# Second MLP product by seven block products (Strassen's algorithm), with the block sums on VectorE and GpSimd and a new order of the work

## The chip, the cores and the metric

One core of a Trainium2 chip. The metric is the device time of one execution in microseconds (us). Weights and inputs come from HBM, the output goes back to HBM, all inside the timed execution.

## The reference

A gated linear attention with 8 heads of 48, followed by a normalisation and a two-layer MLP, over 4 batches of 768 positions, all in float32:

```
B, H, S, D = 4, 8, 768, 48
f = 1 / (1 + exp(-f_logit))
for t in range(S):
    state = f[t] * state + outer(k[t], v[t])     # per batch and head, 48 x 48
    y[t] = q[t] @ state
x = y as (B, S, H*D)                             # 384 columns
xn = (x - mean(x)) / sqrt(var(x) + 1e-6) * g_ln
out = x + maximum(xn @ w_ch1, 0) @ w_ch2         # 384 -> 1536 -> 384
```

Almost all the arithmetic is in the two products of the last line. w_ch1 and w_ch2 arrive as float64 and are turned into float32 in the kernel.

## The kernel before

**Units.** The 768 positions are cut into 12 units of 64 positions. A unit holds these 64 positions of all 4 batches, so 256 rows for the MLP, as two groups of 128 (index g). `attention(n)` and `mlp(n)` are Python generators. A token `a3.scores` in a plan runs the attention of unit 3 up to its stage "scores", a token `m2` runs the next step of the MLP of unit 2, `l3q` issues the loads of q for unit 3. Every engine executes its instructions in the order in which the plan emits them: there is no scheduler, the plan's text alone sets the order. The plan START covers units 0 and 1 with the reading of the weights, and then UNIT is run for m = 2 to 11, which emits the MLP of unit m together with the attention of unit m+1 and the loads of unit m+2.

**The attention of a unit** on TensorE (PE): transposes of f, k and q (`tr`, line 541 in the profile), products with the carried state (`py<-kept`, L615), scores (`ps`, L626), transposes of k (`kp`, L639), products with v (`py<-v`, L649), the new state (`pn`, L674), and the transposes of the normalised rows (`xp`, L703). VectorE (DVE) runs two scans (`after`, `upto`), the products `kh`, `qh`, `kept`, the masked scores `sc`, the statistics `stats`/`mv`, the new `state` and the normalised rows `xn`; GpSimd (POOL) makes the reciprocal deviation `rstd`; ScalarE (ACT) makes the sigmoid `gates` and the copies `kt`, `x`, `xt` out of PSUM.

**The MLP of a unit.** The first product `ph` (L718): for each pair of the 12 blocks of 128 hidden columns, six matmuls with 256 moving columns, and a ReLU on ScalarE into `h` (L720). The second product `po` (L725): for each of the two groups g, twelve matmuls with `h[:, i, g]` as weights and `w2[:, i]` (384 columns) as moving data into one PSUM bank; VectorE then adds x (`o`, L730) and SyncE (SP) issues two stores. In the profile each float32 matmul is recorded as two passes, each with its own weight load (LDWEIGHTS, shown as PEld): 72 matmuls of `ph` and 48 of `po` in a unit.

**The weights.** Each of the 12 pieces (6 of w1, 6 of w2) is fetched by one DMA of 768 KB (token `f`, tile `words`), read by three ScalarE instructions (`r`, L501 to L503, tiles `upper` and `units`), and put together by three VectorE instructions and one GpSimd instruction (`w`, L511 to L518). Pools of rotating buffers: `words` has three, `upper` and `units` two each. PSUM: four single banks, taken in rotation by `tr`, `ph`, `kp`, `po` and `xp`, and two double banks for `py`, `ps` and `pn`. f, q and k have two tiles each, units taking them in turns.

Of the kernel before, what the change touches and what calls it, by code (L numbers as in the profile page):

```python
# [302 lines left out]


START = """
l0v f l0k l0q l0x f l1k l1f a0.gates l1q a0.after a0.k_across a0.upto
a0.k f a0.q a0.scores r a0.causal l1v l1x w a0.kt a0.values r a0.stats
w a1.gates a0.state a0.norm a0.turn m0 r a1.after f a1.k_across f a1.upto
a1.k a1.q w f f r m0 a1.scores a1.causal a1.kt r a1.values
f w w a1.stats r f a1.state m0 m0 r m0 w  # L310
a1.norm l2k a1.turn w m0 m1 r f m1 m1 m1 w
r w r f f r l2f w l3q m1 l2q w
m0 m1 r l2v l2x m0 w a2.gates m1 a2.after m0 m0 a2.k_across
a2.upto a2.k m0 a2.q m1 a2.scores l3k a2.causal l3v l3x l3f a2.kt m1
a2.values m0 a2.stats a2.state m1 a2.norm m1 a2.turn m1
"""
UNIT = """
m{m} a{n}.gates a{n}.after
m{m} a{n}.k_across a{n}.upto
m{m} a{n}.k  # L320
m{m} a{n}.q l{o}f l{o}k l{o}q l{o}v l{o}x
m{m}
m{m} a{n}.scores a{n}.causal a{n}.kt
m{m}
m{m} a{n}.values a{n}.stats a{n}.state
m{m}
m{m} a{n}.norm
m{m} a{n}.turn
m{m}
"""  # L330


# [1 line left out]
def kernel(  # L334
# [58 lines left out]
    def one_bank(name):  # L393
        return ps1.tile([P, 512], FP32, tag="one", name=name)
# [3 lines left out]

    wide_heads = {}
    for name, fill in (("f", 40.0), ("q", 0.0), ("k", 0.0)):  # L400
        for i in range(2):
            t = consts.tile([P, G, H, 64], FP32, name=f"{name}raw{i}")
            nc.gpsimd.memset(t[:, :, :, D:64], fill)
            wide_heads[name, i] = t
    loaded = {}

    def load(n, name, engines=(nc.sync,)):
        if n >= NU:
            return
        if name == "x":  # L410

            loaded[n, name] = raws.tile([P, G, NP, D], FP32, tag="rawx", name=f"vx{n}")
            odd = v.rearrange("b (a r) s d -> b r s a d", r=2)
            for b in range(B):
                nc.sync.dma_start(out=loaded[n, name][(1 - b % 2) * T:(2 - b % 2) * T, b // 2],
                                  in_=odd[b, 1, n * T:(n + 1) * T])
            return
        if name == "v":
            vt = raws.tile([P, G, H, D], FP32, tag="rawv", name=f"v{n}")
            loaded[n, name] = vt  # L420
        else:
            loaded[n, name] = wide_heads[name, n % 2]
        src = {"f": f_logit, "k": k, "q": q, "v": v}[name]
        for b in range(B):
            engines[b % len(engines)].dma_start(  # L425
                out=loaded[n, name][(b % 2) * T:(b % 2 + 1) * T, b // 2, :, 0:D],
                in_=src[b, :, n * T:(n + 1) * T, :].rearrange("h p d -> p h d"))
# [64 lines left out]
    def read():  # L492
# [1 line left out]
        if not fetched:  # L494
            return
        name, words, to, r, w = fetched.pop(0)
        upper = stage.tile([P, r, w], FP32, tag="upper", bufs=2, name=f"{name}upper")
        units = stage.tile([P, r, w], FP32, tag="units", bufs=2, name=f"{name}units")
        wv = words.rearrange("p r (f two) -> p two r f", two=2)
        low, high = wv[:, 0].bitcast(U32), wv[:, 1].bitcast(FP32)  # L500
        nc.scalar.activation(out=upper, in_=high, func=AF.Copy, scale=2.0 ** -112)  # L501
# [17 lines left out]

    pairs = [(g, a) for g in range(G) for a in range(NP)]
    x_of, norm_of, xt_of = {}, {}, {}

    def half(i):
        return slice(64 * i, 64 * i + 64)
# [170 lines left out]
    def turn(n):  # L697
# [8 lines left out]
                              mul=gain[:, m:m + 1])  # L706
        xt_of[n] = xt

    def mlp(n):

        x = x_of.pop(n)
        xt = xt_of.pop(n)
        h = work.tile([P, KF, W], FP32, tag="h", bufs=2, name=f"h{n}")
        for i in range(0, KF, 2):
            ph = one_bank(f"ph{n}").rearrange("p (i t) -> p i t", i=2)
            for j in range(2):
# [2 lines left out]
                                     rhs=xt[:, m], start=m == 0, stop=m == KD - 1)  # L719
            nc.scalar.activation(out=h[:, i:i + 2], in_=ph, func=AF.Relu)  # L720
            yield
        for g in range(G):
            po = one_bank(f"po{n}")[:, 0:DM]
            for i in range(KF):
                nc.tensor.matmul(po, lhsT=h[:, i, g * P:(g + 1) * P], rhs=w2[:, i],  # L725
                                 start=i == 0, stop=i == KF - 1)
                if i % 4 == 3 and i < KF - 1:
                    yield
            o = xs.tile([P, DM], FP32, tag="o", bufs=2, name=f"o{n}")
            nc.vector.tensor_tensor(out=o, in0=x[:, g], in1=po, op=ALU.add)  # L730
            for b in range(2):
                nc.sync.dma_start(out=out[2 * g + b, n * T:(n + 1) * T, :], in_=o[half(b)])
            yield

# [5 lines left out]
    def run(plan):  # L740
        for token in plan.split():
# [9 lines left out]
            elif kind == "m":  # L751
                if token not in running:
                    running[token] = mlp(int(rest))
                next(running[token])
            elif kind == "l":
                load(int(rest[:-1]), rest[-1])
            else:
                {"r": read, "w": write, "f": fetch}[token]()

    run(START)  # L760
    assert not (queue or fetched or opened)
# [48 lines left out]
```

## Time and profile before

| | |
|---|---|
| time, median of 3 runs | 515.3 us (514.0 to 515.7) |
| profiled execution | 515.5 us, its span 513.7 us |
| PE busy | 485.0 us, 94% of the span |
| PEld (weight loads) | 369.7 us, 72% |
| DVE, ACT, POOL busy | 200.7, 129.8 and 41.8 us (39%, 25%, 8%) |
| mean granted TensorE clock | 0.985 |

The busy time of an engine is the union of its instructions. The chain of work that ended last is followed back from the last instruction, at each step to what released it; its shares add up to the span. The table by stretches gives busy times between two points of the span, and the timeline lists instructions in order: start, duration, engine, line, output<-input, shapes, count, and in brackets the idle time of that engine before and what ended it.

### The profile page before, as it was taken

How to read it: one execution, taken by the hardware profiler on the slowest of the kernel's cores; microseconds unless marked ns; L12 is line 12 of the kernel's file. 1: busy time of each engine (PE TensorE's matmuls, PEld its weight loads, DVE VectorE, ACT ScalarE, POOL GpSimd, SP SyncE). 2: the span in 40 equal slices, each digit the busy share in tenths (PEclk: the TensorE clock that was granted, in tenths of full speed). 3: DMA queues.
4: the chain of work that ended last, by engine and by line, in shares of the span. 5: the costliest groups of instructions: out<-in, count | busy, mean ns of one | idle time of the engine just before them, and what ended most of it. 6: DMA issues, size and time to landing. Idle time of an engine off the chain costs nothing.

```text
span 513.7 us, 10940 instructions
## 1 busy us (share of the span) xinstructions
PE 485.0 (94%) x4841; PEld 369.7 (72%) x4841; DVE 200.7 (39%) x285; ACT 129.8 (25%) x255; POOL 41.8 (8%) x53
## 2 busy tenths in 40 slices
PE   2698896999999999999999999999999999999995
PEld 1487783668867867867877876876876876876862
DVE  5879557543432431531521621612603512522000
ACT  3358673012212112212112111221211211211100
POOL 3214326000000000000000000000000000000000
PEclk9969999999999999999999999999999999999999
DMA  9977667433402502602601701700700610000001
GB/s 170 169 197 252 138 155 108 93 63 65 90 14 55 103 3 58 112 3 49 121 3 39 130 4 32 133 7 22 137 14 17 131 25 17 17 1 17 17 1 36
DMA packets 122760, 36.20 MB, mean 70 GB/s; under 512 B 115792, under 2 KB 118864, under 8 KB 122704
## 3 DMA queue, kind: packets, MB, share of 16 engines
q1 hardware_dynamic: 121248, 35.21, 33.9%
q8 instruction: 40, 0.66, 0.5%
q10 hardware_dynamic: 1456, 0.20, 0.3%
q14 instruction: 16, 0.13, 0.1%
HBM read 30.67 MB, written 4.72 MB: 69 GB/s over the span
## 4 chain that ended last, share of the span: by engine, by line
PE 87%; DVE 5%; SPq 3%; issue 1%; ACT 1%; DMA 1%; POOL 1%; DVEq 0%; POOLq 0%
PE po L725 35%; PE ph L718 34%; PE tr L541 6%; SPq L425 3%; PE py L615 2%; PE py L649 2%; PE pn L674 2%; PE ps L626 2%; PE kp L639 2%; PE xp L703 1%; DVE w_0body L514 1%; DMA fraw<-in_f_logit_dram 1%; POOL w L518 1%; DVE w_0body L511 1%; DVE w_0upper L516 1%
## 5 line engine op out<-in xcount | busy, mean ns | idle before, releaser
L725 PE MATMUL po<-w,h 128*128 128x384 f32 x576 | 195.2, 492 | 4.0 <-POOL w L518 4.0
L718 PE MATMUL ph<-xt,w 128*128 128x256 f32 x864 | 195.1, 381 | 0.7 <-ACT xt L705 0.7
L718 PEld LDWEIGHTS ph<-xt,w 128*128 128x128 f32 x864 | 162.8, 191 | 24.3 <-issue 1.1
L725 PEld LDWEIGHTS po<-w,h 128*128 128x128 f32 x576 | 107.4, 191 | 72.8 <-POOL w L518 5.2
L720 ACT ACTIVATE h<-ph 128x512 f32<-128x512 f32 x72 | 42.8, 596 | 166.2 <-PE ph L718 166.2
L730 DVE TENSOR_TENSOR o<-x,po 128x384 f32<-128x384 f32 x24 | 13.3, 554 | 117.6 <-PE po L725 117.6
L555 DVE TENSOR_TENSOR_SCAN after<-gates,ends 128x1040 f32<-128x1040 f32 (+1 forms) x13 | 28.0, 2155 | 35.7 <-ACT gates L574 35.7
L705 ACT ACTIVATE xt<-xp,gain 128x128 f32<-128x128 f32 x72 | 20.0, 375 | 82.9 <-PE xp L703 82.9
L663 DVE BATCH_NORM_STATS2 stats<-x 128x6 f32<-128x384 f32 x24 | 13.0, 543 | 58.9 <-ACT x L659 58.9
L630 DVE TENSOR_TENSOR sc<-ps,causal 128x1024 f32<-128x1024 f32 x12 | 14.7, 1225 | 53.0 <-PE ps L626 53.0
L665 POOL TENSOR_SCALAR rstd<-mv 128x2 f32<-128x2 f32 x12 | 2.8, 234 | 369.0 <-DVE mv L664 368.9
L567 DVE TENSOR_TENSOR_SCAN upto<-gates,starts 128x1040 f32<-128x1040 f32 (+1 forms) x13 | 28.1, 2158 | 0.5
L641 ACT COPY kt<-kp 128x512 f32<-128x512 f32 x24 | 12.9, 589 | 45.1 <-PE kp L639 45.1
L659 ACT COPY x<-py 128x384 f32<-128x384 f32 x24 | 10.3, 482 | 54.1 <-PE py L649 54.1
L593 DVE TENSOR_TENSOR qh<-tr,upto 128x512 f32<-128x512 f32 x24 | 15.6, 686 | 21.0 <-PE tr L541 21.0
L541 PE MATMUL tr<-ident,fraw 128*128 128x128 f32 x96 | 14.7, 298 | 8.5 <-DMA fraw<-in_f_logit_dram 8.5
L541 PEld LDWEIGHTS tr<-ident,fraw 128*128 128x128 f32 x96 | 12.2, 154 | 10.5 <-issue 4.4
L518 POOL TENSOR_TENSOR w<-w_0upper,w_0units 128x768 int32<-128x768 int32 x7 | 15.5, 2212 | 35.5 <-DVE w_0upper L516 19.5
L541 PE MATMUL tr<-ident,kraw 128*128 128x128 f32 x96 | 13.6, 286 | 5.1 <-DMA kraw<-in_k_dram 4.9
L649 PEld LDWEIGHTS py<-v,sc 64*64 64x64 f32 x384 | 12.3, 134 | 7.7 <-issue 6.6
L593 DVE TENSOR_TENSOR kh<-tr,after 128x512 f32<-128x512 f32 x24 | 15.3, 677 | 4.0 <-PE tr L541 4.0
L541 PEld LDWEIGHTS tr<-ident,kraw 128*128 128x128 f32 x96 | 11.7, 148 | 7.1 <-DMA kraw<-in_k_dram 5.3
(90 smaller groups left out, 335.3 us busy)
## 6 DMA issues: line engine op xcount, KB each, us to landing
w_0words<-in_moe_w_ch_dram SPq DMA_DIRECT2D x7, 768.0 KB, 5.2
v<-in_v_dram SPq DMA_DIRECT2D x48, 96.0 KB, 3.0
kraw<-in_k_dram SPq DMA_DIRECT2D x48, 96.0 KB, 3.1
qraw<-in_q_dram SPq DMA_DIRECT2D x48, 96.0 KB, 3.1
out_dram<-o SPq DMA_DIRECT2D x48, 96.0 KB, 2.2
fraw<-in_f_logit_dram SPq DMA_DIRECT2D x46, 96.0 KB, 3.2
vx<-in_v_dram SPq DMA_DIRECT2D x48, 48.0 KB, 2.5
w_256words<-in_moe_w_ch_dram SPq DMA_DIRECT2D x1, 768.0 KB, 5.2
```

What stands on the lines that cost most here:

```text
L425: engines[b % len(engines)].dma_start(out=loaded[n, name][(b % 2) * T:(b % 2 + 1) * T, b // 2, :, 0:D], in_=src[b, :, n * T:(n + 1) * T, : ...
L518: nc.gpsimd.tensor_tensor(out=to.bitcast(I32), in0=upper, in1=units, op=ALU.add)
L541: nc.tensor.transpose(pt[:, a * P:(a + 1) * P], src[:, g, 2 * a:2 * a + 2].rearrange("p h e -> p (h e)"), ident)
L555: nc.vector.tensor_tensor_scan(out=after.rearrange(flat)[:, c0:c1][:, ::-1], data0=gt[:, c0 + 1:c1 + 1][:, ::-1], data1=ends.rearrange(fla ...
L567: nc.vector.tensor_tensor_scan(out=upto.rearrange(flat)[:, c0:c1], data0=gt[:, c0:c1], data1=starts.rearrange(flat)[:, c0:c1], initial=0.0 ...
L593: nc.vector.tensor_tensor(out=dst[:, segs], in0=pt, in1=by[:, segs, 1:E1], op=ALU.mult)
L630: nc.vector.tensor_tensor(out=sc.rearrange("s r e t -> s (r e) t"), in0=ps.rearrange("s r e t -> s (r e) t"), in1=causal.unsqueeze(1).broa ...
L649: nc.tensor.matmul(py[half(b), r, e * D:(e + 1) * D], lhsT=sc[rows, r, e], rhs=vx[rows, g, a] if r else vt[rows, g, 2 * a], start=n == 0 a ...
L705: nc.scalar.mul(out=xt[:, m, g * P:(g + 1) * P], in_=pt[:, m], mul=gain[:, m:m + 1])
L718: nc.tensor.matmul(ph[:, j], lhsT=w1[:, m, (i + j) * P:(i + j + 1) * P], rhs=xt[:, m], start=m == 0, stop=m == KD - 1)
L720: nc.scalar.activation(out=h[:, i:i + 2], in_=ph, func=AF.Relu)
L725: nc.tensor.matmul(po, lhsT=h[:, i, g * P:(g + 1) * P], rhs=w2[:, i], start=i == 0, stop=i == KF - 1)
```

## The change

With h as a 2 x 2 matrix of blocks a11, a12 (group 0, first and second six hidden blocks) and a21, a22 (group 1), and w2 as b11, b12 (first six hidden blocks, left and right 192 columns) and b21, b22, the second product is formed from seven block products in place of eight (Winograd's form of Strassen's algorithm). The sums of weights `mixed` (t1 to t4) are made once, in three parts, on VectorE (token `t`). The sums of h (token `s`: s1, s2, s4, and s3 written over a21) are made for each unit on VectorE. Each product is six matmuls with 192 moving columns (`product`, one PSUM bank each); VectorE adds it, GpSimd adds the partial sums to x, and four tiles of 192 columns (`p1x`, `u4y`, `u4x`, `u2x`) are stored with two DMAs each. f, q and k have one tile each, the pools `raws` and `stage` (with `words`) two buffers instead of three, and START and UNIT are written anew; the MLP of a unit now has 13 steps in place of 12.

```
-    raws = fast.enter_context(tc.tile_pool(name="raws", bufs=3))
-    stage = fast.enter_context(tc.tile_pool(name="stage", bufs=3))
+    raws = fast.enter_context(tc.tile_pool(name="raws", bufs=2))
+    stage = fast.enter_context(tc.tile_pool(name="stage", bufs=2))
...
-            loaded[n, name] = wide_heads[name, n % 2]
+            loaded[n, name] = wide_heads[name]
...
+    def mix():
+        rows = slice(to_mix[0], to_mix.pop(0) + 2)
...
+        for to, x1, x2 in ((t1, b12, b11), (t2, b22, t1), (t3, b22, b12), (t4, t2, b21)):
+            nc.vector.tensor_tensor(out=to, in0=x1, in1=x2, op=ALU.subtract)
...
+    def sums(n):
...
+        nc.vector.tensor_tensor(out=s1, in0=a21, in1=a22, op=ALU.add)
+        nc.vector.tensor_tensor(out=s2, in0=s1, in1=a11, op=ALU.subtract)
+        nc.vector.tensor_tensor(out=a21, in0=a11, in1=a21, op=ALU.subtract)
+        nc.vector.tensor_tensor(out=s4, in0=a12, in1=s2, op=ALU.subtract)
...
-        for g in range(G):
-            po = one_bank(f"po{n}")[:, 0:DM]
-            for i in range(KF):
-                nc.tensor.matmul(po, lhsT=h[:, i, g * P:(g + 1) * P], rhs=w2[:, i],
...
+        def product(name, a, b):
+            pp = one_bank(f"p{name}_{n}")[:, 0:CH]
+            for i in range(KH):
+                nc.tensor.matmul(pp, lhsT=a[:, i], rhs=b[:, i], start=i == 0, stop=i == KH - 1)
+            return pp
...
+        nc.scalar.copy(out=p1, in_=product("p1", a11, b11))
+        add(nc.gpsimd, p1x, p1, x[:, 0, left])
+        yield
+        add(nc.vector, p1x, p1x, product("p2", a12, b21))
+        put(p1x, 0, left)
+        yield
+        s1, s2, s3, s4 = sums_of.pop(n)
+        add(nc.vector, p1, p1, product("p6", s2, t2))
+        add(nc.gpsimd, u2x, p1, x[:, 1, left])
+        yield
+        add(nc.vector, p1, p1, product("p5", s1, t1))
+        add(nc.gpsimd, u4x, p1, x[:, 0, right])
+        add(nc.gpsimd, u4y, p1, x[:, 1, right])
+        yield
+        p7 = product("p7", s3, t3)
+        add(nc.vector, u2x, u2x, p7)
+        add(nc.vector, u4y, u4y, p7)
+        put(u4y, 1, right)
+        yield
+        add(nc.vector, u4x, u4x, product("p3", s4, b22))
...
+        add(nc.vector, u2x, u2x, product("p4", a22, t4), ALU.subtract)
```

**PE, the second product of unit 2 behind the scores of unit 3.** The number after a name's first letters is the unit. Before, from the new state of unit 3 onward:

```order
L674 MATMUL pn3_1419<-v3_1010,kt3_1353 64x48 x32
L725 MATMUL po2_1366<-w2_60,h2_1166 128x384 x4
L725 MATMUL po2_1461<-w2_60,h2_1166 128x384 x8
L703 MATMUL xp3_1474<-ident_58,xn3_1466 128x128 x3
L703 MATMUL xp3_1481<-ident_58,xn3_1466 128x128 x3
L725 MATMUL po2_1461<-w2_60,h2_1166 128x384 x4
```

In the changed kernel, from the product p5 onward:

```order
L753 MATMUL pp5_2_1544<-mixed1_121,s1_2_1466 128x192 x6
L753 MATMUL pp7_2_1560<-mixed3_123,h2_1285 128x192 x6
L683 MATMUL pn3_1571<-v3_1255,kt3_1429 64x48 x32
L753 MATMUL pp3_2_1612<-w2_60,s4_2_1468 128x192 x6
L712 MATMUL xp3_1623<-ident_58,xn3_1609 128x128 x3
L712 MATMUL xp3_1630<-ident_58,xn3_1609 128x128 x3
L753 MATMUL pp4_2_1637<-mixed4_124,h2_1285 128x192 x6
```

Between the new state `pn3` and the transposes `xp3` there were twelve matmuls of 384 columns (four and eight); there is now one product of six matmuls of 192 columns.

**DVE, the same place.** Before, from the masked scores of unit 3 to the second addition of x:

```order
L630 TENSOR_TENSOR sc3_1351<-ps3_1318,causal_111 128x1024
L663 BN_STATS stats3_1408<-x3_1407 128x6
L664 BN_AGGR mv3_1409<-stats3_1408 128x2
L663 BN_STATS stats3_1408<-x3_1407 128x6
L664 BN_AGGR mv3_1409<-stats3_1408 128x2
L679 TENSOR_TENSOR state_126<-kept3_1245,pn3_1419 128x768
L730 TENSOR_TENSOR o2_1457<-x2_1077,po2_1366 128x384
L693 TENSOR_SCALAR xn3_1466<-x3_1407,mv3_1409,rstd3_1410 128x384 x2
L730 TENSOR_TENSOR o2_1492<-x2_1077,po2_1461 128x384
```

In the changed kernel the four sums and the additions of p2 and p6 stand between `sc3` and the first row here:

```order
L761 TENSOR_TENSOR p1_2_1473<-p1_2_1473,pp5_2_1544 128x192
L672 BN_STATS stats3_1539<-x3_1538 128x6
L673 BN_AGGR mv3_1540<-stats3_1539 128x2
L672 BN_STATS stats3_1539<-x3_1538 128x6
L673 BN_AGGR mv3_1540<-stats3_1539 128x2
L761 TENSOR_TENSOR u2x_2_1475<-u2x_2_1475,pp7_2_1560 128x192
L761 TENSOR_TENSOR u4y_2_1477<-u4y_2_1477,pp7_2_1560 128x192
L688 TENSOR_TENSOR state_120<-kept3_1346,pn3_1571 128x768
L702 TENSOR_SCALAR xn3_1609<-x3_1538,mv3_1540,rstd3_1541 128x384 x2
L761 TENSOR_TENSOR u4x_2_1476<-u4x_2_1476,pp3_2_1612 128x192
L761 TENSOR_TENSOR u2x_2_1475<-u2x_2_1475,pp4_2_1637 128x192
```

The statistics now stand behind the addition of p5, and `state` and `xn` behind the two additions of p7.

**SP, the fetches in START.** Before, from the fourth piece of w1 on:

```order
L489 DMA w10_768words_418<-in_moe_w_ch1_dram 128x3x512
L489 DMA w10_1024words_430<-in_moe_w_ch1_dram 128x3x512
L489 DMA w10_1280words_459<-in_moe_w_ch1_dram 128x3x512
L489 DMA w20_0words_461<-in_moe_w_ch2_dram 128x2x768
L489 DMA w22_0words_600<-in_moe_w_ch2_dram 128x2x768
L489 DMA w24_0words_623<-in_moe_w_ch2_dram 128x2x768
L425 DMA kraw0_94<-in_k_dram 64x8x48 x4
L489 DMA w26_0words_742<-in_moe_w_ch2_dram 128x2x768
```

In the changed kernel:

```order
L480 DMA w10_768words_396<-in_moe_w_ch1_dram 128x3x512
L480 DMA w10_1024words_398<-in_moe_w_ch1_dram 128x3x512
L480 DMA w10_1280words_437<-in_moe_w_ch1_dram 128x3x512
L480 DMA w20_0words_568<-in_moe_w_ch2_dram 128x2x768
L416 DMA kraw_90<-in_k_dram 64x8x48 x4
L480 DMA w22_0words_612<-in_moe_w_ch2_dram 128x2x768
L480 DMA w24_0words_614<-in_moe_w_ch2_dram 128x2x768
L416 DMA fraw_86<-in_f_logit_dram 64x8x48 x4
L480 DMA w26_0words_633<-in_moe_w_ch2_dram 128x2x768
```

The order of the pieces is the same; the loads of k and f of unit 2 stand two pieces, respectively three pieces, earlier, and a piece now waits for the piece two before it to be read, where it waited for the piece three before.

More of the change, by code (lines that the diff above doesn't have):

```diff
@@ L713, in mlp @@
         h = work.tile([P, KF, W], FP32, tag="h", bufs=2, name=f"h{n}")
+        h_of[n] = h
         for i in range(0, KF, 2):
@@ L721, in mlp @@
             yield
[L722 to L733 removed]
+        left, right = slice(0, CH), slice(CH, DM)
```

80 lines of the change are left out of this document (50 added, 30 removed).

## The prediction

> **What bounds the kernel now.** I read the table by stretches first: the start, a unit in the middle (unit 3, between its first `ph` and that of unit 4), the unit with the last attention, and the last unit.
>
> ```profile
> core 0: us, PE busy (x) PEld busy (x) DVE busy (x) ACT busy (x) POOL busy (x), PEclk, DMA share, GB/s
> 0.00:120.16 120.16, 98.60 (x1059) 74.08 (x1060) 75.03 (x100) 52.79 (x87) 33.42 (x35) 0.94 0.67 144
> 159.72:199.28 39.56, 39.56 (x415) 30.46 (x415) 13.82 (x20) 8.16 (x18) 0.93 (x2) 1.00 0.30 56
> 476.30:513.70 37.40, 31.02 (x120) 22.45 (x119) 1.53 (x4) 3.58 (x6) 0.00 (x0) 0.97 0.08 19
> ```
>
> From 120 us on TensorE has no gap: 39.56 of 39.56 us, at full granted clock, with VectorE a third busy and GpSimd idle. So a unit costs what its matmuls cost. The start is different: TensorE idles 120.16 - 98.60 = 21.6 us there, while VectorE and ScalarE turn the weights into float32.
>
> The chain of waits gives what one matmul costs when nothing waits, from the last unit, which has no attention beside it.
>
> ```profile
> 476.30 15.54 PE ph L718 x72
> 491.84 15.49 PE po L725 x48
> ```
>
> So 215.8 ns for a pass of 256 columns and 322.7 ns for one of 384: 0.835 ns a column and 2 ns fixed. What a pass of 192 columns costs hangs on whether its weight load still hides, so I looked for the shortest passes that the timeline has with loads of 128 columns.
>
> ```profile
> 274.69 0.49 PE L725 MATMUL po<-w,h 128*128 128x384 f32 x1
> 275.01 0.82 PE L703 MATMUL xp<-ident,xn 128*128 128x128 f32 x6
> 275.56 0.19 PEld L725 LDWEIGHTS po<-w,h 128*128 128x128 f32 x1
> 275.67 0.49 PE L725 MATMUL po<-w,h 128*128 128x384 f32 x1
> ```
>
> Six transposes of 128 columns, each with its own load, take 275.67 - 275.01 = 0.66 us, 110 ns each. And the `po` matmul at 275.67 starts 0.11 us after its own weight load began, though that load is drawn 0.19 us long: the drawn length holds latency that does not delay the next matmul. So a load can follow a load every 110 ns, and 192 columns take longer than that: 110 + 64 x 0.835 = 163 ns.
>
> **The change, part by part.** *The product.* The order shows 42 matmuls of 192 columns, so 84 passes, for the 24 of 384 (48 passes): 84 x 163 ns = 13.69 us against 15.49, 1.80 us less a unit. Bounds: 84 x 160 (0.835 x 192, nothing fixed) is 13.5 us, and 84 x 190, if every load took its drawn length, 16.0 us; I take 163 since both rows above pace at the columns. Over the ten units from 120.16 us on that is 18.0 us, and 3.6 us for units 0 and 1 if the start passes it on.
>
> *VectorE and GpSimd in a steady unit.* Prices are from these groups:
>
> ```profile
> L720 ACT ACTIVATE h<-ph 128x512 f32<-128x512 f32 x72 | 42.8, 596 | 166.2 <-PE ph L718 166.2
> L730 DVE TENSOR_TENSOR o<-x,po 128x384 f32<-128x384 f32 x24 | 13.3, 554 | 117.6 <-PE po L725 117.6
> L630 DVE TENSOR_TENSOR sc<-ps,causal 128x1024 f32<-128x1024 f32 x12 | 14.7, 1225 | 53.0 <-PE ps L626 53.0
> L604 DVE TENSOR_TENSOR kept<-state,total 128x768 f32<-128x768 f32 x11 | 10.5, 952 | 0.0
> L679 DVE TENSOR_TENSOR state<-kept,pn 128x768 f32<-128x768 f32 x10 | 9.2, 922 | 0.0
> L666 POOL TENSOR_TENSOR rstd<-rstd,power 128x2 f32<-128x2 f32 x12 | 9.0, 754 | 1.0
> 72.82 1.84 POOL L518 TENSOR_TENSOR w<-w_0upper,w_0units 128x768 int32<-128x768 int32 x1 [5.93 <-DVE w_0upper L516]
> ```
>
> A sum over h (128x768, both inputs in SBUF) is like `kept`, 0.95 us; four are 3.8. An addition from PSUM of 192 columns, on the slope between `o` and `sc` (671 ns for 640 columns), is 0.35 us; six are 2.1, and the two `o` go (1.1). VectorE gains 4.8 us and stands at 18.6 of 37.8. GpSimd's five additions have no near row; its addition of 128x768 integers, 1.84 us, gives 0.46 us by size, and 0.46 + 0.75 (all of a two-column `rstd` taken as fixed cost) bounds it above; I take 0.6, 3 us a unit on an engine with 0.93. Below nothing it cannot go. ScalarE gains one copy of 192 columns, less than a ReLU's 0.6 us. None of this is on the path unless TensorE waits for it, at three places.
>
> First, p6 needs s2. The last ReLU ends 0.8 us after the last `ph`, and s1 and s2 take 1.9: s2 is there at 2.7, and p1 and p2 keep TensorE until 3.9. Cover 1.2 us, enough also for one GpSimd addition in between. Second, the product with `kept`: before, two blocks of `ph` lay between the transposes of q and it, now one.
>
> ```profile
> 251.67 5.35 PE L718 MATMUL ph<-xt,w 128*128 128x256 f32 x24
> 252.72 0.95 DVE L604 TENSOR_TENSOR kept<-state,total 128x768 f32<-128x768 f32 x1
> 256.94 1.15 PE L615 MATMUL py<-kept,qh 48*64 48x48 f32 x64
> ```
>
> `kept` is done at 253.67, and one block less puts the product at 254.35: 0.7 us are left of 3.3. Third, `xn` before the transposes `xp` (the first row is of the chain of waits, the others of the timeline):
>
> ```profile
> 110.48 1.08 PE pn L674 x64
> 266.37 0.48 ACT L659 COPY x<-py 128x384 f32<-128x384 f32 x1 [5.58 <-PE py L649]
> 266.88 0.56 DVE L663 BATCH_NORM_STATS2 stats<-x 128x6 f32<-128x384 f32 x1 [6.55 <-ACT x L659]
> 268.14 0.18 DVE L664 BATCH_NORM_AGGREGATE mv<-stats 128x2 f32<-128x6 f32 x1
> 268.41 0.22 POOL L665 TENSOR_SCALAR rstd<-mv 128x2 f32<-128x2 f32 x1 [38.55 <-DVE mv L664]
> 268.71 0.71 POOL L666 TENSOR_TENSOR rstd<-rstd,power 128x2 f32<-128x2 f32 x1
> 270.52 0.86 DVE L693 TENSOR_SCALAR xn<-x,mv,rstd 128x384 f32<-128x384 f32 x2
> ```
>
> Count from the end of the products with v (some 0.25 us before the copies, 266.1). The statistics wait for the addition of p5 (done at 2.5) and end at 3.9; GpSimd has finished its two additions by 3.7, and `rstd` is there at 5.0. VectorE adds p7 twice until 4.8, makes `state` from 5.2 (after `pn`, 1.08 us) to 6.1 and `xn` until 6.5 and 7.0. TensorE has p5, p7, `pn` and p3 until 6.9 and asks for the second half at 7.3. It fits, by 0.3 us. I cost it at nothing; what it costs if late is rival two.
>
> *Queues.* SyncE issues eight stores a unit in place of four.
>
> ```profile
> 239.47 1.11 SPq L732 DMA_DIRECT2D out_dram<-o  x2
> 243.49 2.65 SPq L425 DMA_DIRECT2D kraw<-in_k_dram  x4
> kraw<-in_k_dram SPq DMA_DIRECT2D x48, 96.0 KB, 3.1
> ```
>
> The load of k stands behind the stores of u4y and in front of the others. On the count above those stores are issued by 5.9, the loads by 8.6, and k has landed by 12; it is wanted at 15.5, after p3, `xp`, p4, the transposes of f and two blocks of `ph`. The single f, q and k tiles are read early in a unit and filled again behind that: no wait.
>
> *The start.* Rows:
>
> ```profile
> w_0words<-in_moe_w_ch_dram SPq DMA_DIRECT2D x7, 768.0 KB, 5.2
> L489 SPq DMA_DIRECT2D w_0words<-in_moe_w_ch_dram x7: 367/368/627, 5.2 to 71.3; - x7
> 69.53 0.89 ACT L501 ACTIVATE w_0upper<-w_0words 128x768 f32<-128x768 f32 x1
> 70.32 0.91 ACT L502 ACTIVATE w_0units<-w_0words 128x768 f32<-128x768 uint32 x1
> 71.27 0.84 ACT L503 ACTIVATE w_0units<-w_0units 128x768 int32<-128x768 f32 x1
> 84.33 2.32 DVE L555 TENSOR_TENSOR_SCAN after<-gates,ends 128x1040 f32<-128x1040 f32 x1
> 84.56 3.71 POOL L518 TENSOR_TENSOR w<-w_0upper,w_0units 128x768 int32<-128x768 int32 x1 [1.63 <-DVE w_0upper L516]
> 88.32 5.76 PE L725 MATMUL po<-w,h 128*128 128x384 f32 x12 [2.88 <-POOL w L518]
> L725 PE MATMUL po<-w,h 128*128 128x384 f32 x576 | 195.2, 492 | 4.0 <-POOL w L518 4.0
> ```
>
> Before, the last piece is written at 88.3 us and TensorE is dense from there. With two `words` buffers a piece is fetched when the piece two before is read: 2.6 us of reading, 0.4 to issue, 5.2 to land, so 8.2 us for two. I laid the new order out with the durations above. The early part runs 1 to 2 us ahead (k of unit 0 is loaded before the first weights), then scores and weights share VectorE and lose that again; the fifth piece is read at 44 us, the eleventh and twelfth at 73 and 76, and the last is written at 82, GpSimd's slow 3.7 us included, since the mixing runs beside it. Behind it VectorE has a queue: the mixing (twelve subtractions of 384 columns, 0.5 us each, 6 us), the scan of unit 2, its second scan, the additions of p6 and p5, `kh`; p7 needs the bank that `kh` frees, and waits until about 91. From there TensorE has p7, p3, p4 of unit 0 and seven products of unit 1 (10 x 1.95 = 19.5 us) and 6.5 us of attention: the steady part begins at 117 instead of 120.2. So 3.2 us of the 3.6 come through. Bounds: 112.6 if all 3.6 come through and TensorE's 4.0 us of waiting for w2 go too; 132 if all of the 15.8 us of new VectorE work (6.0 mixing, 7.6 sums, 2.2 more additions) came on top of the idle time; I take the laid-out value, near the lower end, since VectorE is idle for 45 of the 120 us now.
>
> *The end.* The last addition is of 192 columns, not 384: 0.2 us.
>
> *Sum.* 513.7 - 18.0 - 3.2 - 0.2 = 492.3 us of span. The profiled execution took 515.5, 1.8 beyond its span, and the median is 0.2 under that: 493.9. I say 494.
>
> **Rivals.** *The weight loads bind (the other side).* If each pass of a product waited for its load's drawn 190 ns, a unit's products would take 16.0 us, 0.5 more than now: 12 x 0.5 less the end's 0.2, about 521. It decides from 15.49 / 84 = 184 ns a pass. Against it stand 110 ns a transpose and the `po` matmul 0.11 us behind its load; for it only that no pass of 192 columns is in the trace. The Trainium skill, "Perfetto Trace Analysis", section "Identifying the Most-Contended Engine", holds that the sum of LDWEIGHTS time over the window, not the matmuls' busy time, says how close TensorE is to its limit. By that rule this change looks full: (72 + 84) x 190 ns = 29.6 us of loads against 29.2 us of matmuls in a unit's MLP. The trace speaks against taking the drawn time as occupancy; on the side of the row, "TensorE: Matmul & The Clock Gate", section "LDWEIGHTS", gives columns / 1.2 ns, 107 ns for 128.
>
> *`xn` or `kept` late.* Between the statistics and `xn` VectorE now has three instructions where it had two, and GpSimd two additions ahead of `rstd`. Even at their upper bound (1.2 us) `rstd` is there at 6.0, when `state` ends. But if the additions are also held up by the two statistics (0.56 us each), it comes at 7.1 and `xn` ends 1 us later: over ten units up to 504, from 0.3 us of delay on. For it: GpSimd and VectorE do hold each other up in the rows above (3.71 for 1.84 us beside a scan). Against it: the statistics read one tile, the scan two.
>
> *The start is bound by VectorE.* If half of its 15.8 us come on the path, the steady part begins at about 124 and the time is 501.
>
> *The start passes on more.* If TensorE no longer waits for w2, the steady part begins at 112.6 and the time is 489.5.
>
> That the change does less arithmetic only on paper is excluded: the order has the 42 matmuls.
>
> **How the numbers follow.** Forecast 0.50 (490.5 to 497.5), a shorter start 0.15 (488 to 490.5), late `xn` or `kept` 0.13, a long start 0.14, loads that bind 0.04, something unseen that takes the gain 0.04. Leaving out the last two, half of the first tail and the top of the late ones, the range is 488 to 503. About 0.3% (1.5 us) is what a measurement here can tell from no change. Faster: all but the last two, with part of the unseen, 0.94; same 0.01; slower 0.05.
>
> **What would show it.** Right: products paced at 163 ns (six matmuls in 1.95 us), a period of 37.8 us, TensorE without gaps from about 117 us, VectorE at about 18.6 us a unit. Wrong: 190 ns a pass; gaps in front of `xp` (released by `xn`), `py<-kept` or p6; a first steady unit after 121 us or before 113; waits of the products in the start for the mixing or for `kh`.

## The result, and the profile after

| | before | after |
|---|---|---|
| time, median | 515.5 us (514.0 to 517.1) | 499.2 us (496.2 to 500.8, 4 runs) |
| ratio | 1 | 0.968, interval 0.962 to 0.973 |
| profiled execution, its span | 515.5, 513.7 us | 498.5, 496.7 us |
| PE, PEld busy | 94%, 72% | 94%, 86% |
| DVE, POOL busy | 200.7, 41.8 us | 270.1, 67.8 us |

The kernel is faster, as forecast, but by 17.0 us of span where 21.4 were forecast. Lines of the code have moved: `ph` is now L741, the products `pp` L753, their additions L761, the sums L725 to L728, the mixing L527, the writing of a weight piece L509, the first scan L564.

The table by stretches for the changed kernel, with the prediction's columns (times, then busy time of PE, PEld, DVE, ACT, POOL, the granted clock, DMA): up to the first `ph` of unit 2, unit 3, and the last unit.

```profile
0.00:119.97 119.97, 97.75 (x1139) 86.18 (x1140) 92.29 (x131) 53.20 (x90) 35.81 (x40) 0.93 0.63 142
158.04:196.12 38.08, 38.08 (x452) 35.19 (x451) 19.09 (x29) 8.58 (x20) 3.29 (x6) 1.00 0.29 54
461.31:496.70 35.39, 29.19 (x157) 27.05 (x155) 6.77 (x13) 3.90 (x7) 2.36 (x4) 0.98 0.07 17
```

A unit in the middle still has TensorE without a gap, 38.08 of 38.08 us, but takes 38.08 where 37.76 were forecast. The last unit takes 35.39 (forecast 37.40 - 1.8 - 0.2 = 35.4). Its own products, by the chain of waits:

```profile
476.85 13.66 PE pp L753 x84
```

84 passes in 13.66 us are 162.6 ns a pass of 192 columns (forecast 163). A group of the page, the weight loads of p6 and p5 (behind the first bar: total us, mean ns):

```profile
L753 PEld LDWEIGHTS pp<-mixed,s 128*128 128x128 f32 x288 | 48.0, 194 | 1.0 <-DVE mixed L527 0.5
```

A load is still drawn 194 ns long on the mean, and yet a pass takes 163, so the next pass does not wait for the whole drawn length.

The 4.4 us that are missing lie in two places. The steady part begins with the transposes of f at 119.1 us (below), 1.1 us ahead of 120.2 before, where 3.2 were forecast: 2.1 us. From there to the last unit it takes 342.2 us against 356.1, a gain of 13.9 where 9 x 1.80 = 16.2 were forecast: 2.3 us. The chain of waits through the start shows how the first came about (start, duration, engine, tile and line of each link).

```profile
67.51 0.97 DVE w_0upper L507
68.61 2.21 POOL w L509
70.84 0.93 ACT w_0upper L492
...
73.73 1.33 POOL p1x L761
75.06 2.11 POOL w L509
77.20 3.12 DVE mixed L527 x3
81.42 0.96 DVE w_0upper L507
82.95 2.92 DVE mixed L527 x3
85.87 2.23 DVE after L564
89.54 6.77 PE pp L753 x40
...
119.09 0.87 PE tr L550 x8
```

Until 89.5 us the chain runs through VectorE and GpSimd, with ScalarE's reading of one piece between: pieces of weights, `p1x`, mixing, scan. TensorE carries it from 89.5. The prediction had p7 wait until about 91; p7 began at 92.2, right behind p6 and p5, and had no wait of its own. The timeline of VectorE and GpSimd there (start, duration) has the prices:

```profile
61.26 2.34 DVE L725 TENSOR_TENSOR s<-h 128x768 f32<-128x768 f32 x1 [0.46 <-ACT h L743]
...
75.03 3.94 POOL L509 TENSOR_TENSOR w<-w_0upper,w_0units 128x768 int32<-128x768 int32 x2
77.20 2.18 DVE L527 TENSOR_TENSOR mixed<-w,mixed 128x384 f32<-128x384 f32 x1 [1.72 <-POOL w L509]
79.30 0.55 DVE L527 TENSOR_TENSOR mixed<-w 128x384 f32<-128x384 f32 x1
...
82.52 2.00 POOL L509 TENSOR_TENSOR w<-w_0upper,w_0units 128x768 int32<-128x768 int32 x1 [3.56 <-DVE w_0upper L507]
82.95 1.99 DVE L527 TENSOR_TENSOR mixed<-w,mixed 128x384 f32<-128x384 f32 x1
```

A step of the mixing costs 0.55 us alone (0.5 forecast), but 2.18 and 1.99 beside GpSimd's writing of a piece, and the first sum of unit 0 costs 2.34, beside the writing of the eighth piece (60.95 to 62.79), where the steady units pay 0.95.

### The profile page after: what moved, and what is told of

Its sections match the earlier page's. It is cut to its first block, busy times and chain, and to the rows that moved or that the text cites. A ratio compares the mean times of both kernels' runs of the same rounds, so it can differ in the third digit from the quotient of the medians.

```text
span 496.7 us, 12128 instructions
## 1 busy us (share of the span) xinstructions
PE 467.8 (94%) x5273; PEld 428.1 (86%) x5273; DVE 270.1 (54%) x405; ACT 133.9 (27%) x267; POOL 67.8 (14%) x98
## 4 chain that ended last, share of the span: by engine, by line
PE 85%; DVE 7%; ACT 2%; DMA 2%; POOL 1%; issue 1%; SPq 0%; DVEq 0%; POOLq 0%; ACTq 0%
PE ph L741 33%; PE pp L753 33%; PE tr L550 5%; PE pn L683 3%; PE py L658 2%; PE py L624 2%; PE ps L635 2%; PE kp L648 2%; DMA fraw<-in_f_logit_dram 2%; DVE mixed L527 2%; PE xp L712 1%; DVE after L564 1%; POOL w L509 1%; ACT w_0upper L492 1%; DVE upto L576 1%
## 5 line engine op out<-in xcount | busy, mean ns | idle before, releaser
L741 PE MATMUL ph<-xt,w 128*128 128x256 f32 x864 | 196.7, 383 | 2.0 <-ACT xt L714 2.0
L741 PEld LDWEIGHTS ph<-xt,w 128*128 128x128 f32 x864 | 162.6, 192 | 23.3 <-ACT xt L714 1.7
L753 PE MATMUL pp<-w,h 128*128 128x192 f32 x288 | 49.8, 328 | 3.9 <-POOL w L509 3.9
L753 PE MATMUL pp<-mixed,s 128*128 128x192 f32 x288 | 52.5, 335 | 0.2 <-DVE mixed L527 0.2
L753 PEld LDWEIGHTS pp<-w,h 128*128 128x128 f32 x288 | 47.3, 190 | 5.4 <-POOL w L509 4.4
L753 PE MATMUL pp<-mixed,h 128*128 128x192 f32 x288 | 50.9, 327 | 0.0
L725 DVE TENSOR_TENSOR s<-h 128x768 f32<-128x768 f32 x12 | 12.9, 1073 | 66.4 <-ACT h L743 66.4
L753 PEld LDWEIGHTS pp<-mixed,s 128*128 128x128 f32 x288 | 48.0, 194 | 1.0 <-DVE mixed L527 0.5
L761 POOL TENSOR_TENSOR p1x<-p,x 128x192 f32<-128x192 f32 x12 | 8.9, 739 | 288.4 <-ACT p L767 288.4
L753 PEld LDWEIGHTS pp<-mixed,h 128*128 128x128 f32 x288 | 46.8, 190 | 0.1
L564 DVE TENSOR_TENSOR_SCAN after<-gates,ends 128x1040 f32<-128x1040 f32 (+1 forms) x13 | 28.9, 2225 | 14.7 <-ACT gates L583 14.7
L761 DVE TENSOR_TENSOR p<-p,pp 128x192 f32<-128x192 f32 x24 | 8.5, 353 | 41.0 <-PE pp L753 40.9
L753 PE MATMUL pp<-w,s 128*128 128x192 f32 x144 | 26.3, 333 | 0.0
L753 PEld LDWEIGHTS pp<-w,s 128*128 128x128 f32 x144 | 23.2, 190 | 0.5
L761 DVE TENSOR_TENSOR u2x<-u2x,pp 128x192 f32<-128x192 f32 x24 | 8.5, 354 | 27.6 <-PE pp L753 27.4
```

Source lines behind the costliest of these rows:

```text
L564: nc.vector.tensor_tensor_scan(out=after.rearrange(flat)[:, c0:c1][:, ::-1], data0=gt[:, c0 + 1:c1 + 1][:, ::-1], data1=ends.rearrange(fla ...
L725: nc.vector.tensor_tensor(out=s1, in0=a21, in1=a22, op=ALU.add)
L741: nc.tensor.matmul(ph[:, j], lhsT=w1[:, m, (i + j) * P:(i + j + 1) * P], rhs=xt[:, m], start=m == 0, stop=m == KD - 1)
L753: nc.tensor.matmul(pp, lhsT=a[:, i], rhs=b[:, i], start=i == 0, stop=i == KH - 1)
L761: engine.tensor_tensor(out=to, in0=x1, in1=x2, op=op)
```

## The experiments

**1. py and pn next to each other.** In UNIT the statistics and the new state move ahead of p5 and p7:

```
-m{m} a{n}.stats m{m} a{n}.state l{o}k a{n}.norm m{m} a{n}.turn m{m}
+a{n}.stats a{n}.state m{m} m{m} l{o}k a{n}.norm m{m} a{n}.turn m{m}
```

> In the middle of each unit the products with v (py), the statistics and the addition to the state (pn) now follow each other with no product between them; p5 and p7 come behind pn. Nothing else changes. Theory of the switch: the unit's 0.32 us over the forecast (38.08 against 37.76) are the price of one more change between the 64-row matmuls of the attention and the 128-row matmuls of the products, since p5 and p7 stood between py and pn (into the 64-row kind 255 ns from start to start where 162 is usual, out of it 148 where 38 is usual, and once in each product behind it 267 where 162 is usual). Then the period falls to 37.77, the ten units lose 3.1 us and the time is 0.994 of the changed kernel's, about 496. Rival: the 0.32 us belong to p5 and p7 themselves (their operands, sums and mixed blocks) or to waits that the records don't show; then the period stays at 38.08 and the time at 499. Second rival: the additions of p7 and xn, which now stand otherwise in VectorE's queue, are late; then a gap on TensorE appears ahead of xp.

The period fell to 37.74 us, in every steady unit. The chain of waits through one unit of the changed kernel, py to the product after pn:

```profile
412.70 1.08 PE py L658 x64
413.78 4.10 PE pp L753 x24
417.88 1.08 PE pn L683 x64
418.96 2.15 PE pp L753 x12
```

and of the experiment:

```profile
412.30 1.08 PE py L658 x64
413.37 0.93 PE pn L683 x64
414.31 6.05 PE pp L753 x36
```

Undisturbed, 24 passes take 3.90 and 12 take 1.95. The products behind a block of 64-row matmuls take 0.20 more, once for each such block, and pn behind a product takes 1.08 where behind py it takes 0.93: 0.35 us for one block more. The median was 497.8, ratio 0.966 (0.964 to 0.968). The time alone does not tell that apart from the changed kernel's 0.968; in the profiled execution the start was 2.0 us later for another reason (see the last section). The period and the chain show the gain.

**2. The same switch added to the kernel before.** Its UNIT with one chunk of `po` between py and pn:

```
-m{m} a{n}.values a{n}.stats a{n}.state
-m{m}
+m{m} a{n}.values a{n}.stats
+m{m} a{n}.state
```

> The kernel before, with one chunk of po (four matmuls) between py and pn in each unit, where they stood next to each other; two chunks follow each other less elsewhere. Nothing of the changed kernel is in it. Theory of the switch: one more change from 64-row to 128-row matmuls and back costs 0.3 us a unit in this kernel too: a period of 39.9 in place of 39.56 and 1.006 of the time before, 518.5. If the 0.34 us belong to the block products, the period stays at 39.56 and the time at 515.4.

Measured 518.4 us, ratio 1.0062 (1.0039 to 1.0085), period 39.91. The chain of waits there:

```profile
425.16 1.08 PE py L649 x64
426.24 2.78 PE po L725 x8
429.02 1.08 PE pn L674 x64
430.10 5.36 PE po L725 x16
```

Eight passes of `po` take 2.78 where 2.58 is usual, sixteen 5.36 for 5.16, and pn 1.08 for 0.93: the same 0.35 us with nothing of Strassen's form in the kernel.

**3. p1x of unit 0 later.** GpSimd's addition moves from p1's step to p2's, for n = 0:

```
-        add(nc.gpsimd, p1x, p1, x[:, 0, left])
+        if n > 0:
+            add(nc.gpsimd, p1x, p1, x[:, 0, left])
         yield
+        if n == 0:
+            add(nc.gpsimd, p1x, p1, x[:, 0, left])
```

> In unit 0 alone GpSimd's addition p1x is emitted in p2's step, behind the last two pieces of w2, instead of in p1's step ahead of them. Theory of GpSimd's queue: in the changed kernel the tenth piece stood ready for GpSimd at 72.3 us but waited until 75.0 behind p1x, which waited for ScalarE's copy of p1; the eleventh and twelfth pieces, p2 and the steady part came later by the same 2 to 2.7 us. Then the last piece is written at 82 instead of 84.5, the steady part begins at 117 instead of 119.1 and the time falls by about 2 us, to 497. Rival: the mixing and the scan on VectorE set the start; then the last piece comes earlier but p6 still begins at about 90 and the time stays at 499.

497.5 us, ratio 0.966 (0.964 to 0.968). The tenth piece was written from 71.7 instead of 75.0, the last from 81.1 instead of 82.5, and the steady part began 1.1 us earlier. But 0.7 us of that was there before the edit could act: the eighth piece was written from 60.2 instead of 61.0 (in the profiles of the changed kernel and its variants it comes anywhere from 58.3 to 62.3). So of the 2.7 us that the tenth piece had waited, some 0.7 reached the last piece and 0.3 the steady part, and the time does not prove even that.

**4. The mixing ahead of the scan.**

```
-w l2q r w m1 t a2.gates m1 w l2v t a2.after
-m0 t a2.k_across ...
+w l2q r w m1 t a2.gates m1 w l2v t t a2.after
+m0 a2.k_across ...
```

> The third step of the mixing stands ahead of the scan of unit 2 on VectorE (from 85.8 us, 2.3 us long), not behind it and behind the addition of p2. Theory of VectorE's queue: p6 waits for the last mixing, which ended at 90.4 us; without the scan and the addition ahead of it it ends at about 87.5, p6 follows p2 nearly at once and the steady part begins about 2 us earlier, at 117: time about 497. Rival: the scan's result is wanted as soon, and the attention of unit 2 comes later by what the product gains; then the time stays at 499.

498.6 us, ratio 0.968 (0.966 to 0.971): nothing. The mixing ended at 87.6 instead of 90.4, and the steady part began at the same time (first `ph` 119.8 in both). The rival was right in its time and wrong in its reason; the wait had moved. From the waits between 84 and 97 us (engine, line, who is waited for: total, times, longest), in the changed kernel and then in this one:

```profile
PE pp L753 <- DVE mixed L527: 0.2, 1, 0.2
```

```profile
PE pp L753 <- DVE p1x L761: 2.2, 1, 2.2
```

p5 now waits for the bank that p2's sum holds, whose addition stands behind the scan.

**5. All three edits.**

> The three edits of this set together: py and pn next to each other, p1x of unit 0 later, the last mixing ahead of the scan. If switch and start theories hold and add up: 3.1 us in the units and 2 to 4.5 us in the start, 491.5 to 494. If the two edits of the start remove the same wait twice: about 494. If neither holds: 499.

495.7 us (495.3 without one run of 502.5), ratio 0.961 (0.959 to 0.964), above the range expected. The period is 37.74, and the first `ph` of unit 2 comes at 119.9, as in the changed kernel: the switch came through, the start's two edits did not. In this profile the eighth piece was 1.5 us earlier than in the changed kernel, and a stretch at half clock (last section) on p5 took about 1.6 us back, so the two cancel.

**6. The scan behind p2's addition too.**

```
-w l2q r w m1 t a2.gates m1 w l2v t t a2.after
-m0 a2.k_across ...
+w l2q r w m1 t a2.gates m1 w l2v t t m0 a2.after
+a2.k_across ...
```

> As the kernel with all three edits, and the scan of unit 2 stands on VectorE behind the addition of p2 as well. In that kernel the mixing was done at 86.2 us, but p5 and p7 still waited until about 90.5, because the bank that they needed was held by p2's sum, whose addition stood behind the scan (86.1 to 88.4). Theory of VectorE's queue: p2's addition now comes at 86.3, p6, p5 and p7 follow each other from about 86 and TensorE is dense about 2.5 us earlier: 493 against 495.7. Rival: the wait moves on once more, to the second scan and the k products (kh) of unit 2, which come 0.3 us later: the same time as all three, 495.7.

495.5 us, ratio 0.961 (0.958 to 0.963): the rival's value. Between 84 and 97 us the products now wait for other additions:

```profile
PE pp L753 <- DVE p L761: 1.1, 2, 0.9
...
PE pp L753 <- DVE p1x L761: 0.3, 1, 0.3
```

Two reorderings of VectorE's queue each removed the wait that they were made for, and each time the next instruction of the same queue took its place.

**7. Less work for VectorE.** First the mixing left out, with blocks of w2 used in place of t1 to t4:

```
-        t1, t2, t3, t4 = mixed
+        t1, t2, t3, t4 = b11, b21, b22, w2[:, 0:KH, right]
```

> The changed kernel without the mixing: p6, p5, p7 and p4 use blocks of w2 as they are, and the twelve subtractions are left out. Nothing else changes. If VectorE's queue behind the last pieces of w2 sets the start, as the prediction's third rival has it, its 6 to 10 us less of work there let p6 follow p2: the steady part begins 3 to 5 us earlier, at 114 to 116, and the time is 494 to 496. If the arrival of the pieces sets it, the gain is that of GpSimd's and VectorE's contention alone, below 1 us: 498 to 499. The period of a unit stays at 38.08.

494.6 us, ratio 0.957 (0.954 to 0.961), first `ph` of unit 2 4.1 us earlier, as the theory of VectorE's queue has it. Then the sums left out, with blocks of h in place of s1 to s4:

```
-        sums_of[n] = s1, s2, a21, s4
+        sums_of[n] = a11, a12, a21, a22
```

> The changed kernel without the four sums over h on VectorE (3.8 us a unit); p6, p5, p7 and p3 use blocks of h as they are. The prediction has these sums wholly beside other work in a steady unit: then the period stays at 38.08 us. If VectorE's access or the wait for s2 costs TensorE something, the period falls, by up to 0.3 us. In the start the sums of unit 0 stand between two pieces of w2: without them the ninth piece is written up to 2 us earlier, which gives 0 to 2 us: 497 to 499 in all.

495.2 us, ratio 0.960 (0.958 to 0.963), first `ph` 3.3 us earlier. Time and `ph` gained more than expected: the ninth piece was written from 62.4 instead of 68.6, the last from 77.5 instead of 82.5. Of that, 2.7 us are not the sums': the eighth piece, ahead of them, was already written from 58.3 instead of 61.0. In both the period stayed at 38.08: beside a steady unit the sums cost nothing. The same row of the chain of waits, where TensorE takes it over for good, without the mixing and without the sums (89.54 in the changed kernel):

```profile
84.38 7.80 PE pp L751 x48
```

```profile
84.55 8.45 PE pp L747 x40
```

In the second, a stretch at half clock (last section) lies on these 40 passes, 8.45 us where the changed kernel's take 6.77. By their medians the two kernels with less work gained 4.6 and 4.0 us on the changed kernel, while the reorderings of experiments 4 and 6 gained 0.6 us and nothing on the kernels that they started from. So VectorE's amount of work ahead of 90 us bound the start; GpSimd's steps lie between on the same chain.

**8. How often a load can follow a load.** `po` of the kernel before in four parts of 96 columns:

```
+                for c in range(0, DM, 96):
+                    nc.tensor.matmul(po[:, c:c + 96], lhsT=h[:, i, g * P:(g + 1) * P],
+                                     rhs=w2[:, i, c:c + 96], ...
```

> The kernel before, with each matmul of po cut into four of 96 columns: the same columns through TensorE, but 192 passes a unit and a weight load for each. It tells how often a weight load can follow another. Theory of the prediction (a load every 110 ns, as in the transposes, whatever the drawn 190): a pass takes 110 ns, a unit's products 21.1 us in place of 15.5, the unit 45.2 and the kernel about 583. If only columns count (96 x 0.835 + 2 = 82 ns): 15.8 us a unit, 519. If the drawn 190 ns bound: 36.5 us a unit, 768.

581.7 us in one run, against 516.1 for the kernel before beside it. Its last unit, by the chain of waits:

```profile
552.19 21.42 PE po L726 x192
```

21.42 / 192 = 111.6 ns a pass, well above the 82 that 96 columns would take and well below the drawn 190: the pace of passes that each bring a load of 128 columns.

**9. Unit 0 with the plain product.** Since VectorE was the bound and TensorE idle in the start, Strassen's form is given up there:

```
+        if n < 1:
+            pos = [one_bank(f"po{n}_{g}")[:, 0:DM] for g in range(G)]
+            for i in range(0, KF, 4):
+                for g in range(G):
+                    for j in range(i, i + 4):
+                        nc.tensor.matmul(pos[g], lhsT=h[:, j, g * P:(g + 1) * P], rhs=w2[:, j], ...
```

> The changed kernel with py and pn next to each other, in which unit 0 alone takes the second product as before: 24 matmuls of 384 columns, in chunks of four matmuls as the pieces of w2 come, and four additions to x; its sums and its seven block products are gone, and the mixing lies behind the first scan of unit 2. TensorE has 1.8 us more to do, VectorE about 5 us less ahead of the last piece. Theory that VectorE's queue bounds the start: the last piece is written at about 79 as without the sums (77.5 + 2.0), TensorE fills its waits with the chunks and the steady part begins at 114 to 117 in place of 119.8: 490 to 493, against 495.7 for the best so far. If TensorE's own work bounds the start, the 1.8 us come on top: 497 to 498.

494.8 us, ratio 0.961 (0.958 to 0.964), first `ph` of unit 2 at 117.4. The last piece was written from 79.5, as expected, but the steady part began a little behind the range, and the time lies between what the two theories gave.

**10. Units 0 and 1 plain.** The same with `n < 2`, and the mixing beside the attention of unit 2.

> As the kernel with unit 0 plain, and unit 1 too; the mixing is done beside the attention of unit 2, where VectorE had half its time free, and first used in unit 2. VectorE is rid of both units' sums (about 9 us) and of the mixing (8 to 10 us with GpSimd's hold-ups) ahead of 100 us; TensorE has 3.6 us more to do. Theory that VectorE's queue bounds the start: from the last piece (about 79) TensorE has 5.2 us of unit 0, 15.5 of unit 1 and about 7 of attention, and the steady part begins at 108 to 112: 485 to 489. If TensorE's own work bounds it: 3.6 us on top, 499. If the sums and the mixing only wait elsewhere (unit 2's p6 waits for the mixing), a gap of some us appears in unit 2's products and the time is 490 to 494.

496.3 us, ratio 0.965 (0.962 to 0.968): the theory as put there failed. From 60.0 to 112.1 us, the changed kernel, unit 0 plain, units 0 and 1 plain (columns as above):

```profile
60.00:112.10 52.10, 47.77 (x434) 44.04 (x435) 41.93 (x55) 17.88 (x30) 15.87 (x13) 0.97 0.43 98
```

```profile
60.00:112.10 52.10, 49.59 (x469) 40.06 (x470) 36.33 (x54) 17.41 (x28) 13.56 (x11) 1.00 0.45 101
```

```profile
60.00:112.10 52.10, 51.85 (x447) 36.84 (x445) 25.86 (x39) 16.45 (x25) 10.58 (x7) 1.00 0.44 100
```

VectorE falls from 41.9 to 25.9 us, and TensorE rises to 51.85 of 52.10: in this stretch TensorE's own work is the bound, from 60 us on. My expectation had counted TensorE's work only from the last piece. But the stretch ends where a gap begins. The chain of waits behind it:

```profile
110.81 0.66 DVE mixed L527 x2
...
114.23 1.30 PE xp L712 x6
115.53 3.82 PE po L751 x8
```

TensorE waited 2.1 us for `xn`, which stood in VectorE's queue behind the mixing, and then a stretch at half clock (last section) made `xp` and eight passes of `po` 1.9 us longer than usual (0.66 and 2.58). Without these 4.0 us the first `ph` of unit 2 would have come at about 116.2, ahead of experiment 9. So the time does not show that TensorE's work alone bounds this start: the third of the expected outcomes, work that only waits elsewhere, came as well, at `xp` and not at p6, and another place for the mixing was not tried.

**11. Unit 0 plain, VectorE's order mended.** The kernel of experiment 9 left TensorE 2.3 us waiting for `kept`:

```
-w l2q r w m0 m0 m1 t a2.gates m1 w l2v t a2.after
-m0 t a2.k_across m0 a2.upto m1 a2.k m1 a2.q l3q s1
+w l2q r w m0 m0 m1 t a2.gates m1 w l2v t t a2.after a2.k_across a2.upto
+m0 m0 a2.k m1 a2.q l3q m1 s1
...
-a2.stats m1 a2.state a2.norm m1 a2.turn l3v m1
+a2.stats a2.state m1 a2.norm m1 a2.turn l3v m1
```

> As the kernel with unit 0 plain; on VectorE the mixing stands ahead of the first scan of unit 2, both scans ahead of the additions of unit 0, and the sums of unit 1 behind kept; on TensorE the transposes of k come ahead of the last chunks of unit 0, and p2 stands between the transposes of q and the product with kept. There VectorE had waited for TensorE between 83 and 92 us (2.86 and 2.33 us busy of 5) and then kept TensorE waiting for kept, 2.3 us. If VectorE's queue is still what holds TensorE back, that gap shrinks to 0.5 us or less and the steady part begins at 115 to 116 in place of 117.4: about 2 us less, 492.5 to 493.5. If TensorE's own work bounds the start by now, the steady part stays at 117.4 and the time at 494.8.

492.3 us, ratio 0.954 (0.952 to 0.957): the fastest of all, 7 us under the changed kernel, and the intervals do not meet. The chain of waits where that gap was:

```profile
98.59 0.89 PE pp L772 x6
99.56 0.87 DVE kept L613
100.99 0.88 DVE s L725
101.89 0.97 DVE s L726
103.00 2.19 PE pp L772 x12
```

The product with `kept` follows p2 with almost no gap; what is left is 0.4 us of waiting for s2. The last line of the edit also puts `py` and `pn` of unit 2 next to each other, which by experiment 1 is worth 0.35 us of the gain. In the profiled execution the pieces came 1.7 us later than in the kernel of experiment 9, and the steady part still began at the same time (117.4), as the gap was gone; the profile by itself shows that much, the comparison of medians (492.3 to 494.8) the rest.

## Why the prediction was right, and where its sizes were off

*The forecast.* 499.2 us lies in the stated range, but above the 490.5 to 497.5 that the prediction gave to its forecast; the range held because it left room for a long start.

*The product.* 84 x 163 ns was right to 0.3% (13.66 against 13.69 us). The loads do not bind at 192 columns; experiment 8 puts their pace at 111.6 ns. The 110 read from the transposes was near it, but did not show it: 128 columns at 0.835 ns and 2 fixed are 109 ns by themselves. The rule of the Trainium skill that was weighed there ("Perfetto Trace Analysis", "Identifying the Most-Contended Engine") would have the loads at 35.19 of 38.08 us a unit as nearly the limit. The trace disagrees: in the last unit the products ran at the pace of their columns.

*The steady unit: 1.80 forecast, 1.48 measured (39.56 - 38.08).* The mis-sized term is the product's place, not its length. I costed the 42 matmuls and left the move of pn, with two products now ahead of it, at nothing, though the order showed it. Before, py and pn stood next to each other; one more block of 64-row matmuls between 128-row ones costs 0.35 us (experiments 1 and 2), which covers the 0.32 missing. The Trainium skill has a rule that fits, in "TensorEngine Tiling (Array Packing)", section "Key Properties": a change of tiling mode drains TensorE. It gives no price there; the runs give 0.35 us for going in and out, and no run here shows that a drain is what takes the time. The prediction did not weigh it.

*VectorE and GpSimd beside a unit.* 19.1 us on VectorE (18.6 forecast) and 3.3 on GpSimd (3.9 forecast), hidden, as the unchanged period without the sums shows. The differences are a miscount: the edit has seven additions on VectorE and four on GpSimd, where six and five were priced; at the prediction's own prices the right counts give 18.9 and 3.3. Of the three margins, two by the timeline:

```profile
256.20 0.96 DVE L726 TENSOR_TENSOR s<-s,h 128x768 f32<-128x768 f32 x1
...
258.28 0.98 PE L753 MATMUL pp<-mixed,s 128*128 128x192 f32 x5
...
267.59 0.86 DVE L702 TENSOR_SCALAR xn<-x,mv,rstd 128x384 f32<-128x384 f32 x2
...
268.63 0.82 PE L712 MATMUL xp<-ident,xn 128*128 128x128 f32 x6
```

s2 is there at 257.16, 1.1 us ahead of p6 (1.2 forecast); `xn` at 268.45, 0.5 us ahead of the second half of `xp`, which follows 0.33 behind 268.63 (0.3 forecast); `kept` has its 0.7 us. The rival of a late `xn` or `kept` did not come.

*The start: 3.2 of 3.6 us forecast to come through, 1.1 did in the profiled pair.* The step that failed is the choice near the lower bound "since VectorE is idle for 45 of the 120 us". That idle time lay elsewhere: from 80 to 90 us VectorE was busy for all but 0.3.

```profile
80.00:90.00 10.00, 7.19 (x33) 6.20 (x33) 9.72 (x14) 1.74 (x4) 2.00 (x1) 0.83 0.03 7
```

Two prices were too low as well. The twelve subtractions took 10.1 us, not 6.0, since two of them ran beside GpSimd and took about 2 us each and a third 0.95, and the first sum 2.34 instead of 0.95; I had used GpSimd's slowed 3.7 us and no slowed VectorE. "SBUF — State Buffer", "Who interferes with whom", in the Trainium skill says the same: a VectorE instruction with two SBUF inputs contends with GpSimd's reads. The laid-out last piece (written at 82) came at 84.5, held up by `p1x` in GpSimd's queue and the sums of unit 0 in VectorE's. And from p7 on TensorE took 26.9 us where 26.0 were counted, 0.6 of it the 0.20 us behind each of three blocks of 64-row matmuls. So the third rival had the right mechanism; with its half of 15.8 us on the path it was too dear (124), and the forecast too cheap.

The 1.1 us are also partly luck of the pair. In the kernel before, half clock lay on the twelve passes of `po` behind the last piece (columns as above):

```profile
88.80:89.60 0.80, 0.80 (x2) 0.36 (x2) 0.00 (x0) 0.00 (x0) 0.00 (x0) 0.50 0.00 0
```

They took 5.76 us, as the prediction's rows show. The kernel of experiment 2 has the same start, had no such stretch, and its chain of waits shows

```profile
89.23 4.14 PE po L725 x12
```

for the same passes. Without the 1.6 us of difference the steady part before would have begun at about 118.5, no later than in the changed kernel. The medians agree: of the 16.3 us between them, 13.9 and 2.0 are the units and the end, so the start gave about 0.4.

*The end:* 2.0 us, as forecast.

## What to carry to other kernels

Cost an added operation in the stretch where it will run: VectorE hid 5 us of new work a unit at no cost in the steady part, and the same kind of work ate most of the saving in the start. While VectorE's whole queue was the bound, a reordering only handed the wait to the next instruction; taking work off the queue helped, even by giving the better algorithm up for one unit, and after that a reordering paid too (experiment 11). And when matmuls are moved, look at the neighbours they part: here one more parting of 64-row blocks cost 0.35 us a unit. Last, compare the start of two profiles only after a look at the granted clock and at a row ahead of the edit.

## What the runs showed of the hardware that was not expected

Going from 128-row matmuls to 64-row ones and back costs 0.35 us, with 0.20 of it in the products behind.

The granted clock falls to 0.50 for a stretch of about 3.4 us at a place that differs between executions. In the changed kernel and in the kernel of experiment 1:

```profile
85.60:89.00 3.40, 3.40 (x14) 3.40 (x13) 3.30 (x5) 0.00 (x0) 0.00 (x0) 0.50 0.02 5
```

```profile
90.70:94.10 3.40, 3.40 (x13) 3.40 (x12) 3.17 (x5) 0.00 (x0) 0.59 (x1) 0.51 0.02 6
```

In the first it lay on p6, which would else have waited for the mixing (written until 90.4), and the start of the kernel without that wait and without such a stretch (experiment 4) was the same; in the second on p5, whose twelve passes took 3.46 us instead of 1.79 from first start to last, and the steady part began 2 us later.

Between 60 us and the last unit, seven of the fourteen profiles have one such stretch: the kernel before, the changed kernel, experiments 1, 3, 5 and 10, and the kernel without the sums. Each begins at the end of a wait of TensorE of 1.9 to 2.9 us, from 0.2 us ahead of that end to 1.0 behind it. Such a wait was not enough by itself: experiments 2, 4, 6 and 9 had waits of 2.2 to 2.9 us and no stretch behind them. The kernels without a wait over 1.4 us there (experiment 11, and that without the mixing) had none either. "TensorE: Matmul & The Clock Gate", "What's actually happening", in the Trainium skill gives half clock after an idle window of some 3.4 us, in windows that run free of the kernel. The length and the changing place agree with it; the idle time does not, since waits of 1.9 to 2.9 us were followed by half clock here.

The stretches are a likely part of the scatter of 1 to 4 us between runs of one kernel. In experiment 9 the three runs with a mean granted clock of 0.987 to 0.990 took 493.3 to 493.6 us, and the three with 0.979 to 0.981 took 496.0 to 496.8; no run was made for it.
